# Moving the gate/up weight copies and the attention steps to other beats of a fused feed-forward and attention kernel

## The chip, the cores and the metric

The kernel runs on one core of a Trainium2 chip. The metric is the device time of one execution in microseconds (us). Before the change it is 1786.29 us, the median of three runs (1786.22 to 1787.94).

## The reference

With S = 2048 rows, D = 576, F = 4608 and 32 heads of 18 channels, the reference computes

```
g   = sigmoid(sum(x * gate_w))                     # one number per row
a   = infini_attention(x, wq, wk, wv, beta) @ wo   # 4 segments of 512 rows: masked softmax + a memory term
b   = (silu(x @ w_gate) * (x @ w_up)) @ w_down     # feed-forward
out = g * a + (1 - g) * b
```

All of it is float32. The kernel splits each operand of its large products into a high and a low part (fp32r) and adds three partial products for each pair. This is why every weight tile needs two instructions before TensorE can use it: a copy of the first term (ACT, `high`) and a subtraction that leaves the second term (DVE, `low`).

## The kernel before

The first 228 us make q, k, v, the memory term and the splits of x. Then follows the main loop, which this document is about, and after it the output projection (from about 1684 us on).

**Units.** The loop in `gated_mix` goes over 72 units: two halves of x (`half`, 0 then 1), and in each half 36 column tiles of 128 columns of gate and up (`f`). A unit makes gate and up for its tile and for two blocks of 512 rows with seven products instead of eight (a Strassen-like scheme). `seven(t, j)` issues product j, six matmuls at L976 and one at L979. The units of a half are called here by q = f mod 3: **q0, q1 and q2**.

**Banks in a unit.** `seven(a, 0)` fills PSUM bank `a`; ACT copies it to bank `xx` (L1033). `seven(y, 1)` fills `y`, which ACT copies out (L1036). `seven(a, 2)` adds to `a`, so TensorE may not begin it before the copy of L1033 has read `a`. DVE forms a new `y` (L1040). `seven(xx, 3)`, then ACT copies `xx` (L1043); `seven(a, 4)`, then ACT copies `a` into `xx` (L1047) and DVE adds (L1048). Then ACT loads the table for Silu, does the two Silu passes (L1050, L1052) and loads the table for Exp again (L969), while TensorE does `seven(y, 5)` and `seven(xx, 6)`. DVE multiplies gate by up (L1057 reads `xx`, L1058). Because `xx` is a single bank, the L1033 of the next unit has to wait for L1057 of this one.

**Beats.** A unit has eight beats, 0 to 7, one after each product and one more between products 5 and 6 (`tick`, which calls `beat`). A beat does three things in this order:

- it issues what was put off to it (`defer`, the list `due`): splits, loads, stores;
- it issues `down_group`s, products with `w_down` at L835, which exist only in q0 units (16 of them, none on beats 0 and 1, then 2, 2, 3, 3, 3, 3); DVE adds each to `ya` (L838, L840);
- it adds to a `credit` (L931) and, at one or more, issues one **attention step** (`att_gen`). `TICK[half][busy]` is the credit for an opportunity, `busy` meaning that down groups are left. In a q0 unit there are 12 opportunities in the eight beats (two each on beats 4 to 7), in a q1 or q2 unit one on each beat that is not in `QUIET`. In half 0 the factor `(half or k > 1)` makes beats 0 and 1 count nothing.

**An attention step** issues work of five stages of a pipeline: a cast on DVE and a subtraction on POOL for step z-3 (`p_bank`, L743 and L744), exponentials on ACT and a mask on POOL for z-1 (`e_bank`, L729 and L737; the three buffers `pe` come free when L744 has read them), scores on TensorE with their maximum on DVE for z (`s_bank`, L711 and L717), a transposing DMA (`x_bank`, L748), and on every fifth step the product with v (`v_unit`, L759, L760). There are 333 steps. When the 334th is asked for, `c_open` releases the attention buffers and starts loading and splitting `wo`, six pieces put off by 1, 2, 4, 5, 8 and 9 beats, with their ACT copy (L868) five beats and their DVE subtraction (L869) seven beats after the load. These pieces use the four `raw` buffers of the gate/up weights.

**Weights.** `w_make(half, f)` plans, in unit f-1, what makes the seven operands of unit f: four sums on POOL (`total`, L243), seven `high` on ACT (L247) and seven `low` on DVE (L250), each on a beat counted from the start of unit f-1 (8 and more fall into unit f). In half 0 the rows of `w_down` are loaded (`d_load`), split by `d_split` on ACT (L918, `dw<-draw`) and one beat later on DVE (L919), and kept in DRAM; half 1 fetches them. `d_split` is called on beats 1 and 7 of q1 units and beat 5 of q2 units. The gated product is split into `hh` (ACT) and `hl` (DVE) on the first beats of the next unit.

Between the halves lies a **break** of ten beats with 16 down groups and no gate/up products. Every engine executes its own instructions in the order in which the code issues them, so the beat decides behind what each one stands. All DMAs are issued by SyncE (SP), in order as well.

Of the kernel before, what the change touches and what calls it, by code (L numbers as in the profile page):

```python
# [40 lines left out]
VL = 8  # L41
KEPT = 2
HALF = ((2, 3), (0, 1))
TICK = ((0.5, 1.0), (0.4, 0.85))
QUIET = (5, 6)
LEAD = 3
SHARE = (0, 0, 2, 2, 3, 3, 3, 3)
BREAK = 10
LOADS = ((-3, 0, 0), (-2, 0, 1), (3, 1, 0), (4, 1, 3), (4, 0, 3), (5, 0, 2), (5, 1, 1), (6, 1, 2))
# [10 lines left out]
def f32(ap):  # L60
    return ap.bitcast(F32)
# [3 lines left out]
def gated_mix(ctx, tc, xT, xrest, wf, wfr, wfh, wd, wv, wo, beta, cmask, ident, bmask, out):  # L65
# [145 lines left out]
    def op_tile():  # L211
        return wop.tile([P, 2, 2, P], F32R, name="wo_")
# [19 lines left out]
    def r_fetch(f):  # L232
        nc.sync.dma_start(f32(rhs[f % 2][:96]).rearrange("p j n -> p (j n)"), rc[f // 4, :, f % 4])

    def w_make(half, f):
        g, u = wraw_of.pop(f)
        ops = wops[half, f] = [None] * 7
        a11, a12, a21, a22 = g[:, 0:2], g[:, 2:4], u[:, 0:2], u[:, 2:4]
        src = [a11, None, None, a12, None, None, a22]

        def total(j, p, q, sub=True):
            src[j] = rp.tile([P, 2, P], F32, name="ws", bufs=3)
            (nc.gpsimd.tensor_sub if sub else nc.gpsimd.tensor_add)(src[j], p(), q())  # L243

        def high(j):
            ops[j] = op_tile()
            nc.scalar.activation(ops[j][:, 0], src[j], AF.Copy)  # L247

        def low(j):
            nc.vector.tensor_sub(ops[j][:, 1], src[j], f32(ops[j][:, 0]))  # L250

        def keep(j):
            nc.sync.dma_start(wc[f, j], f32(ops[j]).rearrange("p a k n -> p (a k n)"))

        todo = [(LEAD - 1, lambda: total(1, lambda: a21, lambda: a22, False)),
                (LEAD, lambda: total(2, lambda: src[1], lambda: a11)),
                (LEAD + 2, lambda: total(4, lambda: a11, lambda: a21)),
                (LEAD + 4, lambda: total(5, lambda: a12, lambda: src[2]))]
        for j in range(7):
            todo += [(LEAD + j, lambda j=j: high(j)), (LEAD + j + 2, lambda j=j: low(j))]  # L260
            if half == 0 and f < KEPT:
                todo.append((LEAD + j + 3, lambda j=j: keep(j)))
        return sorted(todo, key=lambda t: t[0])
# [411 lines left out]
    with ExitStack() as st:  # L675
# [12 lines left out]
        def row_tile():  # L688
            return rw.tile([P, L], F32, name="row")
# [135 lines left out]
        def down_group(c, i, hf, hs, ws, ya, half):  # L825
            b, k = divmod(i, 4)
            cs = (slice(0, 320), slice(320, D))[hf]
            t = pair_tile([P, 320])[:, :cs.stop - cs.start]
            n = 0
            for f in range(CH * c, CH * c + CH):  # L830
                hh, hl = (z[:, b, P * k:P * k + P] for z in hs[half, f])
                d = ws[half, f]
                dh, dl = d[:, 0], d[:, 1]
                for p, q in ((hh, dh), (hh, dl), (hl, dh)):
                    nc.tensor.matmul(t, p, q[:, cs], start=(n == 0), stop=(n == 3 * CH - 1))  # L835
                    n += 1
            if c == 0:
                nc.vector.tensor_copy(ya[:, i, cs], t)  # L838
            else:
                nc.vector.tensor_add(ya[:, i, cs], t, ya[:, i, cs])  # L840
            if c == FT // CH - 1 and hf and half == 0:
                stores.append((ffd[i], ya[:, i]))
# [71 lines left out]
        credit = [-1.0]  # L914
# [6 lines left out]
        def beat(k=None, half=0):  # L921
            for fn in due.popleft() if due else ():
                fn()
            busy = 1 if groups else 0
            share = 2 if k is None else SHARE[k]
            for n in range(max(share, 1)):
                if groups and n < share:
                    down_group(*groups.pop(0))
                if n % 2 or (not busy and (n or k in QUIET)):
                    continue  # L930
                credit[0] += 0.5 if k is None else TICK[half][busy] * (half or k > 1)  # L931
                if credit[0] >= 1:
                    credit[0] -= 1
                    if next(att, att) is att:
                        c_open()

        def feed(half, f):
            return [(f // CH, i, hf, hs, ds, yas[half], half) for i in range(8) for hf in range(2)]
# [45 lines left out]
        for pos, (half, f) in enumerate(seq):  # L984
            if f == 0:
                yas[half] = yp.tile([P, 8, D], F32, name="ya")
            q = f % CH
            nxt = seq[pos + 1] if pos + 1 < len(seq) else None
            if q == 0 and f:
                groups += feed(half, f - 1)  # L990
            plan = []
            if nxt:
                plan += w_fetch(nxt[1]) if nxt[0] and nxt[1] < KEPT else w_make(*nxt)
                if nxt != (0, 1):
                    plan.append((1 if nxt[1] else 10, lambda f=nxt[1]: r_fetch(f)))
                for n, h in enumerate(BLOCKS.get(pos, ())):
                    plan += r_block(h, 4 * n)
                if f + 2 < FT:
                    wraw_of[f + 2] = [None, None]
                    for u in range(2):  # L1000
                        plan.append(((2, 5)[u] if f or not half else 5 + u, lambda u=u, f=f: wraw_of[f + 2].__setitem__(u, w_load(f + 2, u))))
            if pos == FT - 2:
                X2, XR2 = [[None, None] for _ in range(7)], [None] * 7
                plan += [(o + 8, fn) for o, fn in x_second(X2, XR2)]
            for o, fn in plan:
                defer(o + 1, fn)
            step = [0]

            def tick():
                k = step[0]  # L1010
                step[0] += 1
                if k == 0:
                    while stores:
                        nc.sync.dma_start(*stores.pop(0))
                if half == 0:
                    if (q, k) in ((0, 3), (1, 3), (2, 1)):
                        draw[f] = d_load(f)
                    if (q, k) in ((1, 1), (1, 7), (2, 5)):
                        g = f - 1 if k == 1 else f
                        ds[half, g] = d_split(g, draw.pop(g))  # L1020
                elif (q, k) in ((1, 0), (1, 2), (2, 1)):
                    g = f - 1 if k == 0 else f
                    ds[half, g] = d_fetch(g)
                beat(k, half)

            ops, rem = wops.pop((half, f)), rhs[f % 2]
            hh = fp.tile([P, 2, L], F32R, name="hh")
            hl = fp.tile([P, 2, L], F32R, name="hl")
            hs[half, f] = hh, hl
            a, y, xx = a_tile(), y_tile(), x_tile()  # L1030
            p5, sg0, sg1 = (row_tile() for _ in range(3))
            seven(a, 0)
            nc.scalar.activation(xx, a, AF.Copy)  # L1033
            tick()
            seven(y, 1)
            nc.scalar.activation(p5, y, AF.Copy)  # L1036
            tick()
            seven(a, 2, False)
            y = y_tile()
            nc.vector.tensor_add(y, a, p5)  # L1040
            tick()
            seven(xx, 3, False)
            nc.scalar.activation(sg0, xx, AF.Copy)  # L1043
            tick()
            seven(a, 4, False)
            xx = x_tile()
            nc.scalar.activation(xx, a, AF.Copy)  # L1047
            nc.vector.tensor_add(p5, a, p5)  # L1048
            tick()
            nc.scalar.activation(sg0, sg0, AF.Silu)  # L1050
            seven(y, 5, False)
            nc.scalar.activation(sg1, y, AF.Silu)  # L1052
            exp_table()
            tick()
            tick()
            seven(xx, 6, False)
            nc.vector.tensor_mul(sg0, xx, sg0)  # L1057
            nc.vector.tensor_mul(sg1, p5, sg1)  # L1058
            if q == CH - 1:
                defer(2, lambda t=(hh[:, 0], hl[:, 0], sg0): split(*t))  # L1060
            else:
                split_by(2, hh[:, 0], hl[:, 0], sg0)
            split_by(3, hh[:, 1], hl[:, 1], sg1)
            tick()
            assert not groups
            if f == FT - 1:
                groups += feed(half, f)
                if half == 0:
                    for n in range(BREAK):
                        beat(None if n > 1 else n)  # L1070
                    XO, XR = X2, XR2
                    assert not groups
# [98 lines left out]
```

## Time and profile before

| what | us |
|---|---|
| median of three runs | 1786.29 |
| the profiled execution's own time | 1786.73 |
| its span, first to last instruction | 1785.0 |
| main loop begins (first product of unit 0) | 228.06 |
| unit 35 (last of half 0) begins | 941.58 |
| half 1 begins | 986.65 |
| last unit (71) begins | 1671.88 |

Between the profiled execution's time and its span lie 1.73 us. The profile gives, for each engine, busy time and the idle time just before each instruction, with the instruction (or DMA) whose end released it. "PE bank L976 <- ACT bank L1033" is read: TensorE, about to write a bank at L976, was idle until the ACT instruction of L1033 ended. In a list of waits the three numbers are the total, the count and the longest. In a timeline a row gives start, duration, engine, line and operands, and in brackets the idle time before it. Durations of neighbours on ACT and DVE overlap a little, so what an instruction costs its engine is read from the start of the next one.

### The profile page before, as it was taken

How to read it: one execution, taken by the hardware profiler on the slowest of the kernel's cores; microseconds unless marked ns; L12 is line 12 of the kernel's file. 1: busy time of each engine (PE TensorE's matmuls, PEld its weight loads, DVE VectorE, ACT ScalarE, POOL GpSimd, SP SyncE). 2: the span in 40 equal slices, each digit the busy share in tenths (PEclk: the TensorE clock that was granted, in tenths of full speed). 3: DMA queues.
4: the chain of work that ended last, by engine and by line, in shares of the span. 5: the costliest groups of instructions: out<-in, count | busy, mean ns of one | idle time of the engine just before them, and what ended most of it. 6: DMA issues, size and time to landing. Idle time of an engine off the chain costs nothing.

```text
span 1785.0 us, 35149 instructions
## 1 busy us (share of the span) xinstructions
PE 1722.5 (97%) x11868; PEld 1490.2 (83%) x11868; DVE 1345.3 (75%) x3239; ACT 1095.3 (61%) x2201; POOL 933.8 (52%) x1194
## 2 busy tenths in 40 slices
PE   9999999999999999999998999999999999999899
PEld 7898978878878877887887788888888888888699
DVE  6666568788788777877877687888787888877645
ACT  7765575765666576566656656665766576556411
POOL 4433635556655555555555465555565565555121
PEclk9999999999999999999999999999999999999999
DMA  8643487888978887887778967877787778765444
GB/s 290 219 176 134 154 291 176 189 212 183 195 199 186 187 202 181 178 188 188 180 164 238 291 152 162 181 178 157 169 176 178 157 168 190 172 141 139 146 145 140
DMA packets 524004, 328.07 MB, mean 184 GB/s; under 512 B 411184, under 2 KB 460336, under 8 KB 523824
## 3 DMA queue, kind: packets, MB, share of 16 engines
q1 hardware_dynamic: 523824, 325.83, 73.9%
q8 instruction: 93, 1.52, 0.4%
q14 instruction: 87, 0.71, 0.1%
HBM read 165.76 MB, written 76.09 MB: 135 GB/s over the span
## 4 chain that ended last, share of the span: by engine, by line
PE 66%; ACT 15%; DVE 8%; issue 5%; POOL 3%; DMA 2%; SPq 1%; ACTq 0%; DVEq 0%; POOLq 0%
PE bank L976 25%; PE bank L835 18%; PE bank L138 9%; PE bank L979 4%; ACT L969 3%; PE bank L711 3%; ACT L1050 3%; PE bank L759 2%; POOL p L744 2%; ACT pe L729 1%; ACT row L1052 1%; PE bank L760 1%; ACT row L1050 1%; DVE scr L717 1%; PE bank L397 1%
## 5 line engine op out<-in xcount | busy, mean ns | idle before, releaser
L744 POOL TENSOR_TENSOR p<-pe,p 128x512 f16<-128x512 f32 x320 | 375.9, 1175 | 491.2 <-DVE p L743 477.1
L835 PE MATMUL bank<-dw,hh 128*128 128x320 f32 (+1 forms) x2304 | 497.0, 308 | 18.5 <-DVE ya L840 11.4
L835 PEld LDWEIGHTS bank<-dw,hh 128*128 128x128 f32 x2304 | 385.2, 191 | 35.8 <-DVE ya L840 16.5
L729 ACT ACTIVATE pe<-bank,mb 128x512 f32<-128x512 f32 (+3 forms) x512 | 245.8, 521 | 233.6 <-POOL p L744 173.0
L835 PE MATMUL bank<-dw,hl 128*128 128x320 f32 (+1 forms) x1152 | 343.0, 298 | 3.4 <-DVE hl L116 3.4
L717 DVE CUSTOM_DVE_ANT_0 scr<-bank,cm 128x512 bf16<-128x512 f32 (+3 forms) x512 | 247.8, 484 | 6.6
L835 PEld LDWEIGHTS bank<-dw,hl 128*128 128x128 f32 x1152 | 219.5, 191 | 5.7 <-DVE hl L116 5.3
L840 DVE TENSOR_TENSOR ya<-bank,ya 128x320 f32<-128x320 f32 x352 | 157.9, 453 | 80.0 <-PE bank L835 78.5
L979 PE MATMUL bank<-xr,rh 128*128 128x512 f32 x504 | 196.5, 390 | 0.0
L737 POOL TENSOR_SCALAR_AFFINE_SELECT pe<-pe 128x256 f32<-128x256 f32 (+1 forms) x320 | 147.1, 460 | 18.3 <-ACT pe L729 16.7
L743 DVE CAST p<-pe 128x512 f16<-128x512 f32 x320 | 146.9, 459 | 6.8 <-DMA pt<-p 5.9
L243 POOL TENSOR_TENSOR ws<-raw 128x256 f32<-128x256 f32 x140 | 125.8, 899 | 5.8 <-DMA raw<-in_wf_dram 3.5
L711 PE MATMUL bank<-kst,qst 108*128 108x512 bf16 (+3 forms) x512 | 124.8, 305 | 1.7 <-ACT pe L729 1.6
L1043 ACT ACTIVATE row<-bank 128x512 f32<-128x512 f32 x72 | 43.1, 599 | 128.4 <-PE bank L979 128.4
L979 PEld LDWEIGHTS bank<-xr,rh 128*128 128x128 f32 x504 | 94.6, 188 | 20.3
L1047 ACT ACTIVATE bank<-bank 128x512 f32<-128x512 f32 x72 | 41.9, 582 | 96.9 <-PE bank L979 96.9
L919 DVE TENSOR_TENSOR hl<-row,hh 128x512 fp32r<-128x512 f32 x120 | 92.5, 771 | 11.0 <-ACT hh L918 10.9
L1048 DVE TENSOR_TENSOR row<-bank,row 128x512 f32<-128x512 f32 x72 | 49.7, 690 | 64.1 <-ACT bank L1047 64.0
L1050 ACT ACT_TABLE_LOAD x72 | 92.4, 1283 | 1.3
L969 ACT ACT_TABLE_LOAD x72 | 92.4, 1283 | 1.0
L138 PE MATMUL bank<-xo,qhi 128*128 128x512 f32 x264 | 83.1, 396 | 0.0
L353 POOL TENSOR_TENSOR q<-qr,q 128x512 bf16<-128x512 f32 x36 | 44.4, 1234 | 70.6 <-ACT q L352 61.1
(2165 smaller groups left out, 4109.5 us busy)
## 6 DMA issues: line engine op xcount, KB each, us to landing
raw<-in_wf_dram SPq DMA_DIRECT2D x140, 256.0 KB
rh<-rc SPq DMA_DIRECT2D x72, 336.0 KB
dc<-dw SPq DMA_DIRECT2D x36, 576.0 KB
dw<-dc SPq DMA_DIRECT2D x36, 576.0 KB
stk<-q SPq DMA_DIRECT2D x32, 384.0 KB
draw<-in_wd_dram SPq DMA_DIRECT2D x36, 288.0 KB
rc<-rt SPq DMA_DIRECT2D x42, 224.0 KB
vd<-vps SPq DMA_DIRECT2D x8, 912.0 KB
```

The lines of the kernel that those rows point to most:

```text
L138: nc.tensor.matmul(t, st[n], mv[n], start=(n == 0), stop=(n == 13))
L711: nc.tensor.matmul(t[:, c:c + w], qs[:KR, pr, P * i:P * i + P], ks[:KR, pr, 0:w], start=True, stop=True)
L717: nc.vector.tensor_tensor_reduce(scr[:, :w], t[:, c:c + w], cm[:, L - w:L], -SCALE, 3.0e38, OP.add, OP.min, m[:, k:k + 1])
L729: nc.scalar.activation(pe[:, c:c + w], t[:, c:c + w], AF.Exp, bias=m[:, k:k + 1], scale=SCALE)
L737: nc.gpsimd.affine_select(d, d, pattern=pat, compare_op=OP.is_ge, fill=0.0, base=0, channel_multiplier=1)
L743: nc.vector.tensor_copy(p[:, 0], pe)
L744: nc.gpsimd.tensor_sub(p[:, 1], pe, p[:, 0])
L835: nc.tensor.matmul(t, p, q[:, cs], start=(n == 0), stop=(n == 3 * CH - 1))
L840: nc.vector.tensor_add(ya[:, i, cs], t, ya[:, i, cs])
L976: nc.tensor.matmul(t, w[:, p, z], x[z][:, q], start=first and n == 0, stop=False, skip_group_check=True)
L979: nc.tensor.matmul(t, rem[:, RPOS[j]], XR[j], start=False, stop=True, skip_group_check=True)
L1050: nc.scalar.activation(sg0, sg0, AF.Silu)
```

## The change

- Beats of `high` in `w_make`, by operand: 3, 4, 5, 6, 7, 8, 9 before; 2, 3, 3, 7, 7, 8, 9 after. Counted from one, as the change's name counts, these are beats 3, 4, 4, 8, 8, 9 and 10. The beats of `low` stay 5 to 11. The first two `total`s go from beats 2 and 3 to 1 and 2.
- No attention step on beat 7 of a unit without down groups (`QUIET`). Beats 0 and 1 of half 0 now count. The credits change with it.
- `d_split` of q2 units goes from beat 5 to beat 7, its load from beat 1 to 2 (half 0 alone).

From the credits follow the steps of each beat 0 to 7:

```
half 0          before                after
  q0   0 0 1 1 2 2 2 2 = 10    1 0 1 1 2 1 2 2 = 10
  q1   0 0 0 1 0 0 0 1 =  2    0 1 0 1 0 0 0 0 =  2
  q2   0 0 0 1 0 0 0 1 =  2    1 0 1 0 1 0 0 0 =  3
half 1 (before; after it drifts, 10 to 11, 2 and 1 to 2)
  q0   1 0 1 1 2 2 1 2 = 10
  q1   0 1 0 1 0 0 0 0 =  2
  q2   1 0 1 0 0 0 0 1 =  3
steps by the end of half 0: 163 before, 176 after
334th step asked for: unit 71, beat 2 before; unit 70, beat 0 after
```

```diff
-TICK = ((0.5, 1.0), (0.4, 0.85))
-QUIET = (5, 6)
+TICK = ((0.48, 0.85), (0.39, 0.85))
+QUIET = (5, 6, 7)
 LEAD = 3
+HIGH = (2, 3, 3, 7, 7, 8, 9)
+LOW = (5, 6, 7, 8, 9, 10, 11)
...
-        todo = [(LEAD - 1, lambda: total(1, lambda: a21, lambda: a22, False)),
-                (LEAD, lambda: total(2, lambda: src[1], lambda: a11)),
+        todo = [(LEAD - 2, lambda: total(1, lambda: a21, lambda: a22, False)),
+                (LEAD - 1, lambda: total(2, lambda: src[1], lambda: a11)),
...
-            todo += [(LEAD + j, lambda j=j: high(j)), (LEAD + j + 2, lambda j=j: low(j))]
+            todo += [(HIGH[j], lambda j=j: high(j)), (LOW[j], lambda j=j: low(j))]
...
-                credit[0] += 0.5 if k is None else TICK[half][busy] * (half or k > 1)
+                credit[0] += 0.5 if k is None else TICK[half][busy]
...
-                    if (q, k) in ((0, 3), (1, 3), (2, 1)):
+                    if (q, k) in ((0, 3), (1, 3), (2, 2)):
                         draw[f] = d_load(f)
-                    if (q, k) in ((1, 1), (1, 7), (2, 5)):
+                    if (q, k) in ((1, 1), (1, 7), (2, 7)):
```

## Prediction

> **What bounds the kernel now.** I read the page first, then the busy time of the two halves of the main loop, then who waited for whom in each half.
>
> ```profile
> span 1785.0 us, 35149 instructions
> PE 1722.5 (97%) x11868; PEld 1490.2 (83%) x11868; DVE 1345.3 (75%) x3239; ACT 1095.3 (61%) x2201; POOL 933.8 (52%) x1194
> ```
> ```profile
> 228.06:945.00 716.94, 684.87 (x4726) 581.82 (x4724) 567.32 (x1386) 465.96 (x932) 400.12 (x535) 1.00 0.82 193
> 988.00:1670.00 682.00, 676.99 (x4858) 579.55 (x4858) 538.69 (x1330) 432.97 (x869) 381.34 (x488) 1.00 0.76 171
> ```
>
> TensorE (PE) sets the time: it is busy in 1722.5 of 1785.0 us, and neither side of the change adds or removes a matmul. So the time can fall only by PE's idle time and rise only by new idle time. The second fence (stretch, its length, then busy time of PE, weight load, DVE, ACT and POOL) shows where that lies: 716.94 - 684.87 = 32.1 us in the first half, 682.00 - 676.99 = 5.0 us in the second. The halves do the same products; the first one also splits `w_down`.
>
> The waits of the first half (228 to 945 us), then those of the second (988 to 1670 us):
>
> ```profile
> ACT pe L729 <- POOL p L744: 93.4, 47, 3.1
> ACT row L1043 <- PE bank L979: 72.8, 35, 4.6
> DVE dw L919 <- ACT dw L918: 40.6, 11, 3.8
> ACT bank L1047 <- PE bank L979: 40.1, 35, 3.4
> PE bank L976 <- ACT bank L1033: 21.9, 20, 1.3
> ACT bank L1033 <- DVE row L1057: 2.3, 11, 0.3
> ```
> ```profile
> PE bank L976 <- ACT bank L1033: 2.9, 11, 0.5
> ```
>
> Two thirds of the first half's idle time has one cause: 20 times PE stands before product 2 of a unit, because ACT has not yet copied bank `a` (L1033). Yet ACT itself waits for PE in the same units, 72.8 us at L1043 and 40.1 us at L1047. ACT is not short of time, its work stands on the wrong side of L1047. The train from L1047 into a q2 unit, on ACT and then on PE:
>
> ```profile
> 689.52 0.58 ACT L1047 ACTIVATE bank<-bank 128x512 f32<-128x512 f32 x1 [0.29 <-PE bank L979]
> 690.01 0.41 ACT L247 ACTIVATE wo__9026<-ws 128x256 fp32r<-128x256 f32 x1
> 690.44 1.28 ACT L1050 ACT_TABLE_LOAD   x1
> ...
> 694.27 0.40 ACT L247 ACTIVATE wo__9041<-ws 128x256 fp32r<-128x256 f32 x1
> 694.58 0.40 ACT L247 ACTIVATE wo__9047<-raw 128x256 fp32r<-128x256 f32 x1
> 694.89 0.40 ACT L247 ACTIVATE wo__9062<-ws 128x256 fp32r<-128x256 f32 x1
> 695.20 0.67 ACT L918 ACTIVATE dw<-draw 128x576 fp32r<-128x576 f32 x1
> 695.77 0.82 ACT L729 ACTIVATE pe<-bank,mb 128x256 f32<-128x256 f32 x2
> 696.48 0.59 ACT L1033 ACTIVATE bank<-bank 128x512 f32<-128x512 f32 x1
> ```
> ```profile
> 697.13 1.67 PE L976 MATMUL bank<-xo,wo__9041 128*128 128x512 f32 x6 [1.08 <-ACT bank L1033]
> ```
>
> From L1047 to PE's restart pass 697.13 - 689.52 = 7.61 us, and PE by itself needed 7.61 - 1.08 = 6.53. ACT has no gap in it. Into a q0 unit there is one more link, DVE:
>
> ```profile
> 641.08 0.58 ACT L1047 ACTIVATE bank<-bank 128x512 f32<-128x512 f32 x1 [1.49 <-PE bank L979]
> 641.58 0.41 ACT L247 ACTIVATE wo__8322<-ws 128x256 fp32r<-128x256 f32 x1
> 642.00 1.28 ACT L1050 ACT_TABLE_LOAD   x1
> ...
> 647.02 0.40 ACT L247 ACTIVATE wo__8359<-ws 128x256 fp32r<-128x256 f32 x1
> 647.33 0.81 ACT L729 ACTIVATE pe<-bank,mb 128x128 f32<-128x128 f32 x2
> 648.30 0.58 ACT L1033 ACTIVATE bank<-bank 128x512 f32<-128x512 f32 x1 [0.15 <-DVE row L1057]
> ```
> ```profile
> 646.85 0.76 DVE L919 TENSOR_TENSOR dw<-draw,dw 128x576 fp32r<-128x576 f32 x1 [3.79 <-ACT dw L918]
> 647.52 0.68 DVE L1057 TENSOR_TENSOR row<-bank,row 128x512 f32<-128x512 f32 x1
> ```
> ```profile
> 648.93 1.65 PE L976 MATMUL bank<-xo,wo__8338 128*128 128x512 f32 x6 [1.33 <-ACT bank L1033]
> ```
>
> The subtraction of `dw` stands ahead of L1057 in DVE's order and waits 3.79 us for ACT's copy; L1057 runs only at 647.52, and L1033 needs it.
>
> **The change, part by part.**
>
> *Into q2.* Leaving the train: the `high` of beat 4 (690.01 to 690.44, 0.43), one of the three behind it (0.31; two are left on beat 7) and the exponentials of the beat-7 step (695.77 to 696.48, 0.71), in all 1.45. What is left is 6.16 us against PE's 6.53: no stall. The work lands ahead of L1047: a `high` before L1043 (0.31), one more between L1043 and L1047 (0.31), a step's exponentials on beat 1 instead of 7 (0.71). ACT's idle time there, (72.8 + 40.1) / 35 = 3.2 us a unit, covers these 1.3 us. If that cover is gone, L1047 starts late and its excess over 0.37 us comes back as a stall. I leave 0.1 us.
>
> *Into q0.* Leaving: 0.42, 0.31 and the exponentials (647.33 to 648.30, of which 0.15 is the wait for DVE, so 0.82), 1.55 in all; coming in: the exponentials of the new step on beat 4, about 0.7 as above. Of 648.93 - 641.08 = 7.85 us there remain 7.0, against PE's 7.85 - 1.33 = 6.52 plus the score matmuls of the steps now on beats 4 and 0. The `dw` subtraction now follows L1057 (its copy is on beat 7, itself on beat 0), so L1057 starts when product 6 ends. What stalls is between 0 and 0.5 us. I take what the second half shows at the same place, with a step on beat 0 and one on beat 7 there: 2.9 / 11 = 0.26.
>
> The 21.9 us then become about 11 x 0.26 + 11 x 0.1 = 4.0: **-17.9**. Bounds: -21.9, if all of it goes, and -9, if only the part that has a margin (into q2) goes.
>
> *First `total`s a beat earlier.* They need the raw weights, loaded on beat 5 of the unit before, and the third `high` now comes one beat after its sum instead of two. In a short unit POOL has the step's subtraction ahead of it. I cost it at nothing, since POOL is busy 400.12 of 716.94 us there; bounds 0 and, if ACT meets a late sum, the excess over ACT's 3.2 us.
>
> *Down groups after the new beat-0 work.* In q0, DVE now does the `dw` subtraction (0.76 above) and a step's cast and maxima before the first down groups; ACT's `hh` copy comes earlier, since L1033 does. The remaining first-half idle time, 32.1 - 21.9 = 10.2, is unit 0's start and waits for down groups and scores: 0, bounds -4 and +4.
>
> *Break.* Around the last unit of half 0, DVE, ACT and PE:
>
> ```profile
> 958.90 0.68 DVE L1057 TENSOR_TENSOR row<-bank,row 128x512 f32<-128x512 f32 x1
> ```
> ```profile
> 959.61 0.63 ACT L115 ACTIVATE hh<-row 128x512 fp32r<-128x512 f32 x1 [0.70 <-DVE row L1057]
> ```
> ```profile
> 960.30 0.56 PE L835 MATMUL bank<-dw,hh 128*128 128x320 f32 x2 [3.54 <-ACT hh L115]
> 962.41 0.63 PE L835 MATMUL bank<-dw,hl 128*128 128x320 f32 x1 [1.55 <-DVE hl L116]
> ```
>
> PE loses 5.1 us here, because L1057 again stood behind the `dw` subtraction. After the change `hh` waits for ACT alone, which loses the beat-7 exponentials but gets some on beat 4, so it starts about 0.8 earlier; the `dw` subtraction then comes behind `hl` on DVE and is needed one matmul earlier. **-1.1**, bounds 0 and -3.
>
> *Second half.* No `d_split`, one step of beat 7 less, two `high`s less in the train: the 2.9 us go but for 0.4: **-2.5**, bounds -5.0 (all idle time of that half) and +2.
>
> *End.* The waits from 1670 us on, and how they come about:
>
> ```profile
> PE bank L835 <- DVE ya L840: 6.8, 1, 6.8
> ```
> ```profile
> 1688.61 3.68 DMA raw<-in_wo_dram
> ```
> ```profile
> 1678.83 0.42 DVE L250 TENSOR_TENSOR wo__22982<-raw,wo__22982 128x256 fp32r<-128x256 f32 x1
> ```
> ```profile
> 1680.47 0.58 ACT L1047 ACTIVATE bank<-bank 128x512 f32<-128x512 f32 x1 [1.05 <-PE bank L979]
> ```
> ```profile
> 1681.96 1.36 PE bank L976 x6
> ```
>
> PE stops 6.8 us, because the last pieces of `wo` are loaded and split after the loop, ahead of DVE's `ya`. Now they are asked for ten beats earlier. That removes most of the stop, but raises another: the fourth piece takes the `raw` buffer of the last unit's weights, free only after the last `low` (1678.83 + 0.42 = 1679.25). With 3.68 us of load it lands near 1683, and its ACT copy, due on beat 2 of unit 71, stands ahead of L1043 and L1047, which PE's product 6 needs (1681.96, last fence, from the chain). With half a microsecond each for the copy of the piece, L1043 and L1047, product 6 starts near 1684.6: some 2.7 us of new stall. Then `hh` and the first `ya` follow later, too. 6.8 - 2.7 - about 2 for these: **-2.0**, bounds +1 and -6.5.
>
> Sum: -17.9 - 1.1 - 2.5 - 2.0 = -23.5. The profiled execution took 1786.73 us (span 1785.0 and 1.73 around it), 0.44 above the median of 1786.29: 1786.7 - 23.5 = **1763 us**.
>
> **Rivals.**
>
> *ACT is simply full.* The instructions between one L1033 and the next are the same (q1) or one step more (q2). If they fill the unit wherever they stand, 21.9 us stay, and only 1.1 + 2.5 + 2.0 = 5.6 go: 1781. For it: 20 stalls in 24 short units. Against it: ACT's 3.2 us of waiting for PE in each unit.
>
> *All first-half stalls go*, and the halves become alike (32.1 to about 5), with -3, -4 and -6.5 elsewhere: about 1746. For it: the second half shows that this order of work can run with 5.0 us idle. Against it: `w_down` is still split in the first half alone.
>
> *Slower: early steps wait for POOL.* ACT's exponentials wait for a `pe` buffer that POOL's L744 must release, 93.4 / 47 = 1.99 us a time, now mostly in q0 units, where PE has down groups to do. In q2 there will be three steps on beats 0, 2 and 4, just ahead of the copies of L1043 and L1047. If two of them wait so long, 2 x 1.99 less the 1.07 by which L1043's 72.8 / 35 = 2.08 exceeds the moved step and `high` (1.0) makes 2.9 us in 11 units, +32: 1795. It decides when DVE's cast for a beat-0 step comes over a microsecond late. Against it: half 1 has steps on beats 0 and 2 of its q2 units and 5.0 us of idle time in all.
>
> *DVE is slowed by POOL.* A `dw` subtraction that met a POOL subtraction:
>
> ```profile
> 696.61 1.71 DVE L919 TENSOR_TENSOR dw<-draw,dw 128x576 fp32r<-128x576 f32 x1
> ```
>
> That is 0.95 over the 0.76 above. With `dw` on beat 0 next to a new step, and two sums a beat earlier, 11 units could lose it ahead of the down groups: +10.5, 1773. The Trainium skill, "SBUF — State Buffer", section "Who interferes with whom", gives the reason and speaks against the change: a DVE instruction with two SBUF inputs and a GpSimd instruction that reads SBUF exclude each other, and the second waits to the end of the first. By that rule the trace agrees at 696.61 us, not at 646.85, where POOL was idle; the forecast goes by the latter.
>
> **How the numbers follow.** Forecast 0.52, all stalls gone 0.18, ACT full 0.14, POOL and DVE 0.08, slower 0.08. The range that leaves out two in ten reaches from 1748 (the better rival's near side) to 1780 (just short of ACT full). Changes under 0.2% (3.6 us) cannot be told from none. Faster: 0.52 + 0.18 + 0.08 and more than half of ACT full (0.08), 0.86; same 0.06; slower 0.08.
>
> **What would show it.** Right: L976's wait for L1033 in the first half under 8 us, ACT's waits at L1043 well below 72.8, `dw` no longer ahead of L1057, the 3.54 us of the break shorter, a wait of 2 to 3 us in unit 71 with DMA `raw<-in_wo_dram` behind it, and no 6.8 us after it. Wrong: ACT's L729 waiting for POOL in short units, or waits at L835 early in q0 units for `hl` or `dw`.

## The result and the profile after

The kernel after takes **1760.72 us** (median of four runs, 1760.2 to 1762.0) against 1786.74 us of the kernel before (median of four, 1786.22 to 1787.94: the three runs reported above and one more). The ratio is 0.9854, with a 95% interval of 0.9837 to 0.9872. The forecast was 1763.0. The profiled execution took 1760.2 us.

Two lines were added near the top of the file, so a line of the kernel before stands two lines further down in the kernel after: L976 is now L978, L1033 is L1035, L1047 is L1049, L835 is L837. The span and the busy times on the page of the kernel after:

```profile
span 1758.5 us, 35163 instructions
...
PE 1720.8 (98%) x11868; PEld 1482.1 (84%) x11868; DVE 1362.9 (78%) x3239; ACT 1096.9 (62%) x2201; POOL 937.6 (53%) x1194
```

TensorE does the same 11,868 matmuls in nearly the same time. The span is 26.5 us shorter, nearly all of it idle time of TensorE (the table below). Who waited in the first half (228 to 935 us), kernel after:

```profile
ACT pe L731 <- POOL p L746: 99.1, 64, 3.0
ACT bank L1049 <- PE bank L981: 41.1, 34, 2.5
ACT row L1045 <- PE bank L981: 38.4, 24, 3.1
...
PE bank L978 <- ACT bank L1035: 6.6, 11, 0.8
...
DVE dw L921 <- ACT dw L920: 4.8, 11, 0.5
```

The stall that the forecast was about fell from 21.9 us in 20 places to 6.6 in 11. DVE now waits 4.8 us, not 40.6, for the copy of `dw`. The work that ACT now does earlier has filled a part of its wait for TensorE: 38.4 us at L1045, where it waited 72.8. From unit 36 into unit 70 (975 to 1643 us) TensorE's list of waits has one line, and no wait for L1035 is left:

```profile
PE bank L837 <- DVE ya L842: 2.1, 5, 0.9
```

The break, TensorE's timeline in the kernel after (3.54 and 1.55 us before):

```profile
951.70 0.41 PE L837 MATMUL bank<-dw,hh 128*128 128x320 f32 x1 [2.51 <-ACT hh L117]
953.09 0.64 PE L837 MATMUL bank<-dw,hh 128*128 128x320 f32 x1 [0.98 <-DVE dw L921]
```

And TensorE's waits from unit 71 to the end, kernel after:

```profile
PE bank L837 <- ACT hh L117: 1.7, 1, 1.7
PE bank L837 <- DVE ya L842: 0.6, 1, 0.6
PE bank L978 <- ACT bank L1035: 0.4, 1, 0.4
PE bank L837 <- DVE hl L118: 0.3, 1, 0.3
```

The 6.8 us for `ya` are down to 0.6, and the stall of 2.7 us that the forecast put into unit 71, ahead of product 6, has not come: only 0.4 us are there, ahead of product 2. The table adds up TensorE's idle times of the timeline (the numbers in brackets ahead of each matmul), from the first product of unit 0 on:

| TensorE idle, us | before | after |
|---|---|---|
| unit 0 | 2.4 | 3.0 |
| products, q2 units of half 0 | 10.3 | 1.1 |
| products, q0 units of half 0 | 12.6 | 6.9 |
| down groups and scores, q0 units of half 0 | 7.8 | 6.3 |
| break | 5.8 | 4.4 |
| half 1 up to unit 71 | 5.0 | 2.3 |
| unit 71 to the end | 8.2 | 3.0 |
| all | 52.0 | 27.0 |

### The profile page after: what moved, and what is told of

It reads as the page before. It is cut to its first block, busy times and chain, and to the rows that moved or that the text cites. A ratio compares the mean times of both kernels' runs of the same rounds, so it can differ in the third digit from the quotient of the medians.

```text
span 1758.5 us, 35163 instructions
## 1 busy us (share of the span) xinstructions
PE 1720.8 (98%) x11868; PEld 1482.1 (84%) x11868; DVE 1362.9 (78%) x3239; ACT 1096.9 (62%) x2201; POOL 937.6 (53%) x1194
## 4 chain that ended last, share of the span: by engine, by line
PE 66%; ACT 11%; DVE 11%; issue 4%; DMA 3%; POOL 3%; SPq 1%; POOLq 0%; DVEq 0%; ACTq 0%
PE bank L978 23%; PE bank L837 22%; PE bank L140 9%; PE bank L981 4%; PE bank L713 3%; PE bank L761 2%; DVE hl L921 2%; ACT L971 2%; DVE scr L719 2%; ACT L1052 2%; DVE p L745 1%; PE bank L762 1%; ACT pe L731 1%; DMA pt<-p 1%; POOL p L746 1%
## 5 line engine op out<-in xcount | busy, mean ns | idle before, releaser
L746 POOL TENSOR_TENSOR p<-pe,p 128x512 f16<-128x512 f32 x320 | 377.4, 1179 | 479.2 <-DVE p L745 455.5
L837 PE MATMUL bank<-dw,hh 128*128 128x320 f32 (+1 forms) x2304 | 490.8, 306 | 15.2 <-DVE ya L842 8.4
L837 PEld LDWEIGHTS bank<-dw,hh 128*128 128x128 f32 x2304 | 378.2, 189 | 38.9 <-DVE ya L842 19.7
L837 PE MATMUL bank<-dw,hl 128*128 128x320 f32 (+1 forms) x1152 | 340.4, 296 | 0.3 <-DVE hl L118 0.3
L837 PEld LDWEIGHTS bank<-dw,hl 128*128 128x128 f32 x1152 | 217.8, 189 | 0.6 <-DVE hl L118 0.6
L739 POOL TENSOR_SCALAR_AFFINE_SELECT pe<-pe 128x256 f32<-128x256 f32 (+1 forms) x320 | 147.8, 462 | 12.6 <-ACT pe L731 9.4
L745 DVE CAST p<-pe 128x512 f16<-128x512 f32 x320 | 142.7, 446 | 6.5 <-DMA pt<-p 6.5
L245 POOL TENSOR_TENSOR ws<-raw 128x256 f32<-128x256 f32 x140 | 120.3, 860 | 24.6 <-DVE wo__22862 L252 4.1
L921 DVE TENSOR_TENSOR hl<-row,hh 128x512 fp32r<-128x512 f32 x120 | 111.1, 926 | 10.6 <-ACT hh L920 10.4
L1045 ACT ACTIVATE row<-bank 128x512 f32<-128x512 f32 x72 | 43.1, 599 | 87.9 <-PE bank L981 87.9
L1049 ACT ACTIVATE bank<-bank 128x512 f32<-128x512 f32 x72 | 41.9, 582 | 82.6 <-PE bank L981 82.2
```

What stands on the lines that cost most here:

```text
L739: nc.gpsimd.affine_select(d, d, pattern=pat, compare_op=OP.is_ge, fill=0.0, base=0, channel_multiplier=1)
L745: nc.vector.tensor_copy(p[:, 0], pe)
L746: nc.gpsimd.tensor_sub(p[:, 1], pe, p[:, 0])
L921: defer(k + 1, lambda: nc.vector.tensor_sub(lo, src, f32(hi)))
```

## The experiments

Each kernel was run beside the kernel before on one chip, and ratios are to that. TensorE's busy time differs by up to 10 us between these profiles (1717.9 to 1727.4) though its instructions are the same, so the idle times stand beside the times.

### Each part alone

The change falls into three edits. The first moves the first terms (and the two sums):

```diff
+HIGH = (2, 3, 3, 7, 7, 8, 9)
+LOW = (5, 6, 7, 8, 9, 10, 11)
...
-        todo = [(LEAD - 1, lambda: total(1, lambda: a21, lambda: a22, False)),
-                (LEAD, lambda: total(2, lambda: src[1], lambda: a11)),
+        todo = [(LEAD - 2, lambda: total(1, lambda: a21, lambda: a22, False)),
+                (LEAD - 1, lambda: total(2, lambda: src[1], lambda: a11)),
...
-            todo += [(LEAD + j, lambda j=j: high(j)), (LEAD + j + 2, lambda j=j: low(j))]
+            todo += [(HIGH[j], lambda j=j: high(j)), (LOW[j], lambda j=j: low(j))]
```

> Kernel before with the new beats of high and the two earlier sums alone. Train theory (what stands behind L1047 on ACT counts, instruction by instruction): 0.74 us leaves the train, so the stall into q2 goes from about 1.0 to 0.3 us and into q0 from 1.3 to 0.6, since the dw copy on beat 5 and with it L1057 come earlier too; the first half's L976 wait for L1033 falls from 21.9 to about 10 us, and the time to about 1775. Rival (ACT is full, the order does not matter): the wait stays at 20 to 22 us and the time at 1786.

The second has the step rule alone:

```diff
-TICK = ((0.5, 1.0), (0.4, 0.85))
-QUIET = (5, 6)
+TICK = ((0.48, 0.85), (0.39, 0.85))
+QUIET = (5, 6, 7)
...
-                credit[0] += 0.5 if k is None else TICK[half][busy] * (half or k > 1)
+                credit[0] += 0.5 if k is None else TICK[half][busy]
```

> Kernel before with the new credits and quiet beats alone. Train theory: into q2 the beat-7 exponentials (0.7 us) leave, 1.0 becomes 0.3; into q0 the dw subtraction still stands ahead of L1057 on DVE, and the exponentials now on beat 4 come before it, so that stall grows from 1.3 to 1.6 us: the first half's L976 wait stays near 20 us. The end gives about 5 us and the second half 2.5, so about 1778. Rival (the three parts add, each with its share): about a third to a half of the 26 us here, with the L976 wait falling to 12 or less.

The third has the split of `w_down` and its load alone:

```diff
-                    if (q, k) in ((0, 3), (1, 3), (2, 1)):
+                    if (q, k) in ((0, 3), (1, 3), (2, 2)):
...
-                    if (q, k) in ((1, 1), (1, 7), (2, 5)):
+                    if (q, k) in ((1, 1), (1, 7), (2, 7)):
```

> Kernel before with the split of w_down in q2 units on beat 7 instead of 5 (load on beat 2) alone. Train theory: L1057 no longer waits for the dw copy, but ACT has the same instructions ahead of L1033, so into q0 only the 0.15 us goes by which L1033 waited for DVE: L976 wait 20 us instead of 21.9; the stall of 3.5 us in the break becomes about 2.5. Time about 1783. Rival (DVE is the last link into q0): 11 stalls of 1.3 us go, L976 wait near 10, time about 1772.

### Each part left out

The same three edits, each taken back out of the kernel after. Without the moved first terms (the two sums go back as well):

```diff
...
-            todo += [(HIGH[j], lambda j=j: high(j)), (LOW[j], lambda j=j: low(j))]
+            todo += [(LEAD + j, lambda j=j: high(j)), (LEAD + j + 2, lambda j=j: low(j))]
```

> Kernel after with high on beats 3 to 9 and the sums on 2 and 3 as before. Train theory: 0.74 us comes back into each train: into q2 from 0 to about 0.3 us, into q0 from 0.6 to 1.3; L976 wait of the first half 17 to 19 us instead of 6.6, time about 1772. Rival (the steps alone do it): L976 wait under 9, time 1761 to 1764.

Without the step rule:

```diff
-TICK = ((0.48, 0.85), (0.39, 0.85))
-QUIET = (5, 6, 7)
+TICK = ((0.5, 1.0), (0.4, 0.85))
+QUIET = (5, 6)
...
-                credit[0] += 0.5 if k is None else TICK[half][busy]
+                credit[0] += 0.5 if k is None else TICK[half][busy] * (half or k > 1)
```

> Kernel after with the credits and quiet beats of before. Train theory: beat-7 exponentials (0.7 us) back in the train, into q2 0.3 us, into q0 about 0.5 (no step on beat 4, so two effects nearly cancel there); L976 wait about 9 us; end as before (8 us idle), second half 1 to 3 us worse. Time about 1771. Rival (steps do most of it): L976 wait near 20, time about 1780.

Without the later split:

```diff
-                    if (q, k) in ((0, 3), (1, 3), (2, 2)):
+                    if (q, k) in ((0, 3), (1, 3), (2, 1)):
...
-                    if (q, k) in ((1, 1), (1, 7), (2, 7)):
+                    if (q, k) in ((1, 1), (1, 7), (2, 5)):
```

> Kernel after with the split of w_down in q2 units on beat 5 as before. Train theory: into q0 the chain dw copy, dw subtraction, L1057, L1033 is again as long as ACT's own train, stall 0.7 to 1.1 us instead of 0.6; the break's first stall back from 2.5 to over 3.5 us. L976 wait 8 to 12 us, time 1763 to 1767. Rival (this part gives nothing): 1761.

What the six measured (idle times of TensorE, from the timelines; "into" means the products of that kind of unit in half 0):

| kernel | time, us | ratio to before, interval | into q2 | into q0 | half 1 | unit 71 on | idle, all |
|---|---|---|---|---|---|---|---|
| before | 1786.7 | 1 | 10.3 | 12.6 | 5.0 | 8.2 | 52.0 |
| first terms alone | 1775.3 | 0.9928 (0.9912 to 0.9945) | 4.0 | 6.3 | 2.2 | 8.2 | 38.2 |
| steps alone | 1783.0 | 0.9977 (0.9964 to 0.9989) | 5.4 | 19.4 | 5.0 | 3.4 | 44.1 |
| split alone | 1780.2 | 0.9959 (0.9944 to 0.9974) | 10.3 | 9.4 | 5.0 | 8.3 | 47.1 |
| without first terms | 1769.8 | 0.9910 (0.9893 to 0.9926) | 5.4 | 8.8 | 5.0 | 3.5 | 33.8 |
| without steps | 1765.2 | 0.9887 (0.9872 to 0.9901) | 4.0 | 3.8 | 2.3 | 7.9 | 32.3 |
| without split | 1771.2 | 0.9918 (0.9904 to 0.9933) | 1.1 | 17.5 | 2.3 | 2.7 | 36.4 |
| after | 1760.7 | 0.9854 (0.9837 to 0.9872) | 1.1 | 6.9 | 2.3 | 3.0 | 27.0 |

Four things can be read in the columns.

- Into q2 the two edits that shorten ACT's train add up: 10.3, less 6.3 for the first terms, less 4.9 for the step rule, which takes the exponentials off beat 7, and with both only 1.1 is left. The split plays no part.
- Into q0 the first terms and the split help beside any of the others. **The steps hurt**: 6.8 us by themselves, 11.2 beside the first terms (6.3 to 17.5), 3.1 beside both (3.8 to 6.9). Only beside the split alone they cost nothing (9.4 to 8.8).
- The gain in half 1 comes from the first terms alone: with the steps or the split by themselves 5.0 us stay.
- The gain from unit 71 on comes from the step rule alone.

Three expectations missed the size of the stalls: with the split left out the stalls are 18.6 us (1.1 + 17.5) and with the steps alone 24.8 (5.4 + 19.4), both more than was expected; without the first terms they are 14.2 (5.4 + 8.8), which is less. The time without the steps was missed too, 1765 us where about 1771 was expected: half 1 got no worse and into q0 less was lost. Why the split matters so much beside the new steps is seen in DVE's and ACT's timelines of the kernel without the split, at the place where the forecast showed the kernel before:

```profile
645.17 0.76 DVE L921 TENSOR_TENSOR dw<-draw,dw 128x576 fp32r<-128x576 f32 x1 [2.14 <-ACT dw L920]
645.84 0.68 DVE L1059 TENSOR_TENSOR row<-bank,row 128x512 f32<-128x512 f32 x1
```
```profile
644.46 0.67 ACT L920 ACTIVATE dw<-draw 128x576 fp32r<-128x576 f32 x1
...
646.62 0.58 ACT L1035 ACTIVATE bank<-bank 128x512 f32<-128x512 f32 x1 [0.87 <-DVE row L1059]
```

ACT has become quick enough to wait 0.87 us for DVE. The link through the `dw` subtraction now sets the end, and whatever makes ACT's copy of `dw` late (the exponentials of the step on beat 4, ahead of both Silu passes) goes straight into TensorE's stall.

### What is left into q0

In the kernel after, ACT's, POOL's and TensorE's timelines at the same place:

```profile
634.03 0.58 ACT L1049 ACTIVATE bank<-bank 128x512 f32<-128x512 f32 x1 [0.57 <-PE bank L981]
635.10 0.84 ACT L731 ACTIVATE pe<-bank,mb 128x256 f32<-128x256 f32 x2 [0.49 <-POOL p L746]
635.96 1.28 ACT L1052 ACT_TABLE_LOAD   x1
...
640.41 0.67 ACT L920 ACTIVATE dw<-draw 128x576 fp32r<-128x576 f32 x1
640.98 0.57 ACT L1035 ACTIVATE bank<-bank 128x512 f32<-128x512 f32 x1
```
```profile
633.90 1.17 POOL L746 TENSOR_TENSOR p<-pe,p 128x512 f16<-128x512 f32 x1 [0.97 <-DVE p L745]
```
```profile
641.61 1.21 PE L978 MATMUL bank<-xo,wo__8481 128*128 128x512 f32 x4 [0.47 <-ACT bank L1035]
```

From L1049 to TensorE's restart pass 641.61 - 634.03 = 7.58 us; TensorE itself needed 7.58 - 0.47 = 7.11. In ACT's train stand the exponentials of the step on beat 4, and ahead of them ACT waits 0.49 us for a `pe` buffer, which POOL's L746 releases at 633.90 + 1.17. Without that wait the train would take 7.09 us, and the stall would be gone here. This is one of six q0 units that lose 0.46 to 0.48 us. The other five lose 0.73 to 0.80 (0.80 in unit 18, behind the same wait of 0.49), because TensorE needs about 0.3 us less there; in these the wait is not all of the stall. So the next kernel makes beat 4 quiet as well, with credits that keep the number of steps; the third step of a q2 unit falls on beat 3, and those of q1 on beats 1 and 2:

```diff
-TICK = ((0.48, 0.85), (0.39, 0.85))
-QUIET = (5, 6, 7)
+TICK = ((0.6, 0.85), (0.49, 0.85))
+QUIET = (4, 5, 6, 7)
```

> Kernel after with beat 4 quiet too and credits 0.6 and 0.49: in q2 units of the first half steps on beats 0, 2, 3 instead of 0, 2, 4, in q1 units on 1, 2 instead of 1, 3. If the 0.5 to 0.8 us still lost into q0 come from the exponentials on beat 4 (0.86 us on ACT and a wait of 0.49 us for POOL ahead of the Silu table): L976 wait from 6.6 to under 2 us, time about 1756. If what is lost is set elsewhere, or steps 1.6 us apart make ACT wait for DVE's maxima ahead of L1047: no gain, 1761 to 1768.

It took 1769.2 us, a ratio of 0.9910 (0.9895 to 0.9925), longer than the kernel after. Into q0 the stall halved, but another one came. TensorE's waits of its first half:

```profile
PE bank L978 <- ACT bank L1049: 9.1, 11, 0.9
PE bank L837 <- DVE ya L842: 5.1, 12, 1.8
PE bank L978 <- ACT bank L1035: 3.3, 11, 0.3
```

The new stall of 0.85 us stands ahead of product 6 of the q2 units, and ACT's and TensorE's timelines name it:

```profile
451.31 0.84 ACT L731 ACTIVATE pe<-bank,mb 128x256 f32<-128x256 f32 x2 [1.66 <-POOL p L746]
452.03 0.60 ACT L1049 ACTIVATE bank<-bank 128x512 f32<-128x512 f32 x1
```
```profile
452.68 1.66 PE L978 MATMUL bank<-xo,wo__5688 128*128 128x512 f32 x6 [0.85 <-ACT bank L1049]
```

Two steps on neighbouring beats leave POOL no time between them: the second one's exponentials wait 1.66 us for POOL, now ahead of L1049. This is the forecast's "early steps wait for POOL", at 0.85 us a unit instead of 2.9.

The other way is to take the third step out of q2 units. A table fixes the steps of half 0: q0 gets eleven, q1 and q2 two each.

```diff
+PLAN = ((1, 1, 1, 1, 2, 1, 2, 2), (0, 1, 0, 1, 0, 0, 0, 0), (1, 0, 1, 0, 0, 0, 0, 0))
...
-                credit[0] += 0.5 if k is None else TICK[half][busy]
+                credit[0] += 0.5 if k is None else TICK[1][busy] if half else (PLAN[q][k] > n // 2) * 1.0
```

> The kernel after, except that in half 0 the steps follow a table: q0 1 1 1 1 2 1 2 2 (eleven, one more, on beat 1), q1 on beats 1 and 3 as before, q2 only on beats 0 and 2 (its third step, on beat 4, is gone). If the 6.9 us that are left into q0 come from that step's exponentials in the train (theory), they fall to about 3.3, as in the run with beat 4 quiet, and the 10.8 us into q2 of that run do not come, because they came from its steps on neighbouring beats (1 and 2 of q1, 2 and 3 of q2), whose exponentials wait for POOL. The waits in q0 for down groups (6.3) stay. About 1757. Rival: any step moved into q0 costs there what it saves, since q0 already holds ten; waits at down groups grow by 3 or more, about 1761 or above.

1769.67 us, 0.9908 (0.9891 to 0.9924). The stall into q0 is gone altogether, and so is the one of the run before; into q2 some of 0.3 us have come (2.5 us in all). But the rival was right as well: the down groups pay. TensorE's waits of the first half, and DVE ahead of one of them (one line was added, so `ya` is L843 here):

```profile
PE bank L838 <- DVE ya L843: 15.6, 11, 1.5
```
```profile
646.77 0.63 DVE L746 CAST p<-pe 128x512 f16<-128x512 f32 x1
647.32 0.41 DVE L720 CUSTOM_DVE_ANT_0 scr<-bank,cm 128x256 bf16<-128x256 f32 x1
...
650.14 0.48 DVE L843 TENSOR_TENSOR ya<-bank,ya 128x320 f32<-128x320 f32 x1
```
```profile
650.67 0.56 PE L838 MATMUL bank<-dw,hh 128*128 128x320 f32 x2 [1.54 <-DVE ya L843]
```

The cast and the maxima of the step on beat 1 stand ahead of the `ya` of beat 2. So the eleventh step goes to beat 5, and the credit starts at -1.2, by which the steps end on the beat on which they end in the kernel after:

```diff
-PLAN = ((1, 1, 1, 1, 2, 1, 2, 2), (0, 1, 0, 1, 0, 0, 0, 0), (1, 0, 1, 0, 0, 0, 0, 0))
+PLAN = ((1, 0, 1, 1, 2, 2, 2, 2), (0, 1, 0, 1, 0, 0, 0, 0), (1, 0, 1, 0, 0, 0, 0, 0))
...
-        credit = [-1.0]
+        credit = [-1.2]
```

> As the run with eleven steps in q0, but the eleventh on beat 5 instead of beat 1 (q0: 1 0 1 1 2 2 2 2), and the steps end on the same beat as in the kernel after (unit 70, beat 0). Theory: the 11.4 us more at the down groups of that run came from DVE's first product with ya, late behind casts, maxima and splits of a step on beat 1; on beat 5 nothing of that stands in the way. Into q0 0 us as there, down groups about 6 as in the kernel after, unit 71 on about 3: 20 us idle in all, about 1754. Rival: DVE has no room for an eleventh step anywhere in q0; the down groups pay 5 us or more on another beat, 1759 or above.

**1749.02 us** (1746.25 to 1751.41), a ratio of 0.9788 (0.9774 to 0.9803). This beats both kernels. TensorE is idle 18.0 us in all, 6.8 in half 0 behind unit 0. Its waits of the first half:

```profile
PE bank L838 <- DVE ya L843: 3.8, 11, 1.1
...
PE bank L979 <- ACT bank L1036: 0.2, 1, 0.2
```

Of the wait for ACT's copy of bank `a` (now L1036), 21.9 us in the kernel before, 0.2 are left, and the down groups wait no longer than in the kernel after.

### The end

The kernel after, with `c_open` called at the fourth request past the last step instead of the first, on beat 2 of unit 71 as in the kernel before:

```diff
                     if next(att, att) is att:
-                        c_open()
+                        ended.append(k)
+                        if len(ended) > 3:
+                            c_open()
```

> Kernel after, but the buffers of the attention are released and wo is loaded only at the fourth request after the last step, on beat 2 of the last unit as before the change; steps and everything else stay. If the earlier loads are what shortened the end: PE's idle time after the last unit begins returns from 3.0 to about 8 us, time about 1766. If the end was shortened by the steps being over two units early: it stays near 3 us and 1761.

1768.58 us, 0.9893 (0.9878 to 0.9908). Idle time from unit 71 on is 8.5 us instead of 3.0, elsewhere within 0.5 us of the kernel after in each part. TensorE's waits there:

```profile
PE bank L837 <- DVE ya L842: 7.2, 1, 7.2
```

So the early `c_open`, and nothing else, removes the long stop. Then the change without its step rule, but with credits by which the steps of half 1 end in unit 69:

```diff
-TICK = ((0.48, 0.85), (0.39, 0.85))
-QUIET = (5, 6, 7)
+TICK = ((0.5, 1.0), (0.42, 0.88))
+QUIET = (5, 6)
...
-                credit[0] += 0.5 if k is None else TICK[half][busy]
+                credit[0] += 0.5 if k is None else TICK[half][busy] * (half or k > 1)
```

> The change without its step rule (as in the run without the steps: 1765.2, 32.3 us idle), but with credits of 0.42 and 0.88 in half 1, so that the last step is asked for in unit 69 instead of 71. If the step rule gives only the early end (theory), the 7.9 us idle from unit 71 on fall to about 3, total idle about 27, about 1760, as the kernel after. Rival: the steps' places in half 0 are worth something by themselves, or more steps in half 1 cost there what the end gives: 1763 or more.

1771.34 us, 0.9912 (0.9897 to 0.9927): the rival's side. The idle time from unit 71 on fell only to 5.1, and half 1 rose from 2.3 to 5.5 with the steps that were pressed into it. In the 5.1 us is a wait that the kernel after lacks:

```profile
PE bank L981 <- DMA rh<-rc: 2.8, 1, 2.8
```

It also stood in the run with beat 4 quiet (2.2 us) and in the first one with a table (2.5). In all three the steps end in unit 69. The last run therefore repeats the fastest kernel with the credit starting at -1.0, which ends the steps one beat earlier:

> The same with the credit starting at -1.0 instead of -1.2, so that the last step is asked for one beat earlier (unit 69, beat 7). Theory, from the three runs in which the steps ended in unit 69: the first wo piece then stands ahead of the last rh load in SP's order, and TensorE waits 2 to 3 us for rh at product 0 or 1 of unit 71; about 2 to 3 us longer than the run beside it. Rival: that wait came from something else in those runs, and one beat makes no difference.

```diff
-        credit = [-1.2]
+        credit = [-1.0]
```

1762.12 us, 0.9870 (0.9854 to 0.9887). The wait came, as expected. SP's queue in the fastest kernel, then SP's and TensorE's timelines in this one:

```profile
1628.61 0.49 SPq L236 DMA_DIRECT2D rh<-rc  x1
1629.31 0.60 SPq L868 DMA_DIRECT2D raw<-in_wo_dram  x1
```
```profile
1639.55 7.15 SPq L868 DMA_DIRECT2D raw<-in_wo_dram  x2
...
1647.90 0.42 SPq L236 DMA_DIRECT2D rh<-rc  x1
```
```profile
1653.58 0.50 PE L982 MATMUL bank<-xr,rh 128*128 128x512 f32 x1 [2.40 <-DMA rh<-rc]
```

With the steps ending one beat earlier, two `wo` loads stand ahead of the last `rh` load in SP's order, and SP is held by the second for a buffer (7.15 us for the two). In the fastest kernel `rh` goes out 0.7 us ahead of the first piece.

But this wait is 2.4 us of a difference of 13.1 between the medians, so the expectation missed the size. The two profiled executions differ by 11.1. Of these, 6.6 are idle time: 2.1 more from unit 71 on, 5.1 in q2 units and 1.7 in the break, and 2.3 less elsewhere. The other 4.6 us are busy time (1717.9 to 1722.5). The shift of one step has moved the every-fifth product with v: with 15 steps in three units it falls on the same beats all the way, here three times into a q0 unit, in the faster kernel twice into q0 and once into q1. That the phase causes the q2 waits was not tried by itself, and where the extra busy time comes from stays open. The phase also differs between the two runs with eleven steps in q0 before this one, beside the beat of the eleventh. Here, with a third phase and the eleventh step on beat 5, q0's down groups wait 3.9 us (4.7 in the fastest kernel, 17.7 with the step on beat 1). So two phases with the step on beat 5 cost little, which speaks for the beat, not the phase, as what they pay for; beat 1 was not tried with another phase.

## Why the prediction came out right, point by point

**Into q2: right in mechanism, the equal number by chance.** 1.1 us were forecast, 0.1 in each unit, and 1.1 measured, but not in the same stalls. Those for ACT's copy of bank `a` are gone from all the q2 units. What is there is one new stall, of unit 35, ahead of product 4, for DVE's addition at L1042:

```profile
942.01 0.69 DVE L1042 TENSOR_TENSOR bank<-bank,row 128x512 f32<-128x512 f32 x1
```
```profile
942.75 1.65 PE L978 MATMUL bank<-xo,wo__12897 128*128 128x512 f32 x6 [1.09 <-DVE bank L1042]
```

The parts that the forecast took out of the train show up one by one: the first terms by themselves take 6.3 us, the step rule by itself 4.9.

**Into q0: right direction, too little cost.** The forecast left 2.9 us (0.26 a unit) and 6.9 are there. The mis-sized term is the exponentials that come in on beat 4, "about 0.7": in the unit shown they hold ACT 0.86 us, and ACT also waits 0.49 us ahead of them for POOL. So the train took 7.58 us, not 7.0. The forecast had this wait as a rival, placed before L1045 and L1049 at 2.9 us a unit; it stood behind L1049, at less than 1. The step rule, which the forecast credited with a gain here, costs 3.1 us beside the other two edits and 6.8 by itself. The gain into q0 belongs to the first terms and the split.

**Break: right. Second half: right number, one cause of three.** The forecast had -1.1 and -2.5; the table shows -1.4 and -2.7. In the break both waits fell as described (3.54 to 2.51, 1.55 to 0.98). For the second half the forecast named the missing `d_split`, one step of beat 7 less and two `high`s less. The `d_split` sets this half apart from the first and is no part of the change, and with the step rule by itself all 5.0 us stay: the moved `high`s did it (2.2 with the first terms alone). The 2.9 us of waits for ACT's copy of bank `a` went altogether.

**First sums a beat earlier, down groups: right.** Both were put at nothing. ACT met a late sum in two places in the first half, 0.7 us each; the sums were not tried by themselves. Waits of q0's down groups went from 6.1 to 6.3 us; the waits for scores there (1.7 us) went to nothing.

**End: the removal right, the new stall wrong.** The forecast took back 4.7 of 6.8 us, because the fourth `wo` piece would take the last unit's raw buffer. But the fourth piece did not wait for that buffer. SP's timeline, and DVE's last `low` of unit 71, in the kernel after:

```profile
1655.75 1.23 SPq L867 DMA_DIRECT2D raw<-in_wo_dram  x2
...
1661.36 0.55 SPq L867 DMA_DIRECT2D raw<-in_wo_dram  x1
```
```profile
1660.88 0.42 DVE L252 TENSOR_TENSOR wo__23012<-raw,wo__23012 128x256 fp32r<-128x256 f32 x1
```

The third and fourth loads go out back to back from 1655.75 to 1656.98, over four microseconds before the last `low` ends (1661.30); by the times, the fourth took the buffer of the first piece. It is the sixth that goes out alone at 1661.36, right behind that `low`, and its copy is due after L1049, so it doesn't stand ahead of product 6. The gain was 5.2 us instead of 2.0. A stall of the forecast size does exist one beat away, by another resource: SP's order, with `rh` behind the pieces.

**The rivals.** "ACT is full" is refuted by the column "into q2": work that only changes its place takes those stalls away. "All first-half stalls go" did not happen in this change, but the fastest kernel, with 1749.0 us, comes near its 1746. "Early steps wait for POOL" came in small, as said above. "DVE is slowed by POOL" did not come as described. DVE's two subtractions at L919 in the kernel before, and the same at L921 after (shortest, median and longest in ns):

```profile
L919 DVE TENSOR_TENSOR hl<-row,hh x120: 675/692/1768, 246.4 to 1687.3; 128x512 fp32r<-128x512 f32 x120
...
L919 DVE TENSOR_TENSOR dw<-draw,dw x36: 748/758/1711, 248.9 to 958.2; 128x576 fp32r<-128x576 f32 x36
```
```profile
L921 DVE TENSOR_TENSOR hl<-row,hh x120: 677/806/1657, 246.3 to 1668.1; 128x512 fp32r<-128x512 f32 x120
L921 DVE TENSOR_TENSOR dw<-draw,dw x36: 749/758/1292, 249.9 to 952.3; 128x576 fp32r<-128x576 f32 x36
```

`dw` itself did not get slower; the subtraction of `hl` did, by 114 ns in the median. The down groups did not pay for it (6.1 and 6.3 us, above). The Trainium skill, "SBUF — State Buffer", section "Who interferes with whom", states that a DVE instruction with two SBUF inputs contends with a GpSimd instruction that reads SBUF; the longer `hl` agrees with that, but no run here held POOL still to show it.

The sum, -23.5 us, stands against -25.0 us of idle time and -26.0 of the medians. Two errors, 4.0 us too much gain into q0 and 3.2 too little at the end, nearly cancel. That the forecast came so near, 1763 against 1760.7, is luck to that extent.

## What to carry to other kernels

An engine that waits in one place and is late in another has its work on the wrong side of an instruction that others need: compare its waits with the train behind that instruction, and move what can run earlier. A moved step brings its buffers along, so its price is the instruction plus the wait for the buffer (0.86 and 0.49 us here), and two steps on neighbouring beats paid more than two steps apart (a wait of 1.66 us). When a loop's end is brought forward, follow the in-order DMA queue: here one beat decided whether the last load of the loop stood ahead of the new ones or behind them.

## What the runs showed of the hardware

TensorE's busy time for the same 11,868 matmuls lay between 1717.9 and 1727.4 us in these profiles. That is more than several of the effects studied here, so a part of a change is better read from idle times by place than from one time. Three edits that save 13.8, 7.9 and 4.9 us of idle time alone save 25.0 together, close to their sum of 26.6, although into q0 they are far from independent: the split saves 3.2 us there alone and 10.6 beside the other two (17.5 to 6.9).
